# Constants staged and two padding tiles: SBUF start offsets in a fused attention and two-MoE kernel

## The chip, the cores and the metric

One core of a Trainium2 chip runs the whole program. The metric is device time in microseconds (us), the median of three runs.

## The reference

Three steps follow one another on 4608 tokens of 512 features.

```python
# attention: 8 batches x 8 heads, 576 positions of 64 features, softmax inside chunks of 64 positions
attn = softmax(q_c @ k_c.T / 8) ; x = (attn @ v_c)          # x: 4608 x 512
# first MoE: 8 experts 512 -> 1024 -> 512, one expert per token, only tokens with x @ w_skip > 0
e = argmax(x @ w_gate) ; x += gate * (relu(x @ w1[e]) @ w2[e])
# second: dense, 512 -> 2048 -> 512; its weights come as float64
h = x @ w_in ; g = where(h >= 1, h, where(h <= -1, 0, (h + 1)**2 / 4)) ; out = g @ w_out
```

## The kernel before

**Attention and routing** work through 18 units of 256 tokens: q, k and v are loaded by SyncE's DMA queue (`load_qk`, `load_v`), transposed and multiplied on TensorE, and the rows of x are written to DRAM (`xn` to `x_dram`) with a list of tokens for each expert.

**The first MoE** goes expert by expert. An expert's weights come in eight pieces of 128 x 1024 (`piece`): loaded into a staging tile `stg`, then split by ScalarE and VectorE (some by GpSimd) into a high and a low float32r tile. Experts at even places use the pool `wa` (tiles `ah0` to `ah7`, `al0` to `al7`), those at odd places the pool `wb` (`bh*`, `bl*`). `s_M1` makes the hidden features: the weights are the stationary operand, the tokens (`xh`, `xl`) the moving one, 256 to 384 columns of it. `s_M2` makes the output: the hidden features are stationary, the weights move, 512 columns each. In `s_M2` a block of 128 tokens takes 24 matmuls: eight blocks f of hidden features, for each of them (hh, wh), (hh, wl), (hl, wh) as (stationary, moving). The hidden features of f 0 to 3 lie in the pool `h0` (`hh0`, `hl0`, `hh1`, `hl1`), those of f 4 to 7 in the pool `h1` (`hh2` to `hl3`).

**The second MoE** takes nine groups of 512 tokens and for each group 16 blocks m of 128 hidden features. `mm_A` (12 matmuls, output `a`) has the weights `ah*`, `al*` as stationary and the tokens `xh`, `xl` as moving operand; `s_B` (12 matmuls, output `b`, two blocks behind) has the features `gh`, `gl` as stationary and the weights `bh*`, `bl*` as moving operand. ScalarE and VectorE make g of the block in between. In the first group each block also carries one `decode` of a piece of `w_out` from its float64 bits, on VectorE (L189 to L199) and ScalarE.

All matmuls are issued by the helper `mm` (L135) or `tr` (L138), in program order. In a row of the profile `a<-xl,ah` is a matmul into tile a with the operands xl and ah; `mm(o, l, r)` has l as stationary and r as moving operand.

**Where tiles lie.** Pools lie one behind another in each partition of SBUF, in the order in which they are opened, from byte 16512 on; a tile takes a multiple of 32 bytes, and the tile of a closed pool makes room for the next one. The small tiles of the pool `const` come first, among them `cst` (the constants as float32, 677 columns) and `cb` (the first 544 of them as bf16). So the size of `const` sets where every larger tile starts. The rows inside a weight tile, a token tile of 256, 384 or 512 columns and a feature tile are multiples of 512 bytes apart, so that what one matmul reads starts at the same place past a multiple of 512 as its tile.

Of the kernel before, what the change touches and what calls it, by code (L numbers as in the profile page):

```python
# [21 lines left out]
P = 128  # L22
# [64 lines left out]
def kernel(ctx, tc, q, k, v, w_skip, w_gate, w1, w2, w_in, w_out, consts, out):  # L87
# [9 lines left out]
    dec_p = ctx.enter_context(tc.tile_pool(name="dec", bufs=2))  # L97
    ps_moe = ExitStack()
# [8 lines left out]
    cst = const.tile([P, C_ID], F32, name="cst")  # L107
# [13 lines left out]
    ident = const.tile([P, P], F32, name="ident")  # L121
    iota = cb[:, C_IOTA - C_TRI:C_SEL - C_TRI]
# [17 lines left out]
    # ------------------------------------------------ weights  # L140
# [8 lines left out]
    def piece(e, j):  # L149
        """a piece of an expert's weights: loaded, then split"""  # L150
        if j < KD:
            src = w1.rearrange("e (k p) f -> p (e k) f", p=P)[:, bass.ds(ids[e] * KD + j, 1), :]
        else:
            src = w2.rearrange("e (f p) d -> p (e f) d", p=P)[:, bass.ds(ids[e] * (F1 // P) + 2 * (j - KD), 2), :]
        st = stg_p.tile([P, 1024], F32, tag="stg", name="stg")
        halves = [slice(0, 512), slice(512, 1024)]
        for i, cut in enumerate(halves):
            nc.sync.dma_start(out=st[:, cut], in_=src[:, 0, cut] if j < KD else src[:, i])
        yield
        hi, lo = w_t[e, j] = pair(e, j)  # L160
        for cut in halves:
            nc.scalar.copy(out=hi[:, cut], in_=st[:, cut])  # L162
        for cut in halves:
            (nc.vector if e or j == 7 else nc.gpsimd).tensor_tensor(out=lo[:, cut], in0=st[:, cut], in1=hi[:, cut], op=ALU.subtract)  # L164

    # the second half of the hidden features' columns of w_in is split early and waits in DRAM
    m2w = tc.dram_tile([KD, 2, P, 1024], F32R, name="m2w")

    def decode(nm, n, keep=False):
        """a piece of the second MoE's weights: float64 bits into two float32r parts"""  # L170
        if nm == "in":
            kk, c = n % KD, n // KD
            src = w_in[kk * P:kk * P + P, c * 512:c * 512 + 512]
            j, half = kk * 2 + c // 2, c % 2
        else:
            src = w_out[n * P:n * P + P, :]
            j, half = n // 2, n % 2
        cut = slice(half * 512, half * 512 + 512)
        st = (kst_p if keep else stg_p).tile([P, 1024], I32, tag="stg", name="stg")
        nc.sync.dma_start(out=st, in_=src.bitcast(I32))  # L180
        if keep:
            yield
        yield
        v2 = st.rearrange("p (n t) -> p n t", t=2)
        low, top = v2[:, :, 0], v2[:, :, 1]
        a = dec_p.tile([P, 512], I32, tag="a", name="a")
        s = dec_p.tile([P, 512], I32, tag="s", name="s")
        af, sf = a.bitcast(F32), s.bitcast(F32)
        nc.vector.tensor_scalar(out=a, in0=top, scalar1=3, scalar2=0x3FFFFFFF, op0=ALU.logical_shift_left, op1=ALU.bitwise_and)  # L189
        nc.vector.scalar_tensor_tensor(out=a, in0=top, scalar=masks[:, 0:1], in1=a, op0=ALU.bitwise_and, op1=ALU.bitwise_or)  # L190
        nc.vector.tensor_scalar(out=s, in0=a, scalar1=masks[:, 1:2], scalar2=None, op0=ALU.bitwise_and)  # L191
        if keep:
            hl = st.bitcast(F32).rearrange("p (t n) -> p t n", t=2)
            hi, lo = hl[:, 0].bitcast(F32R), hl[:, 1].bitcast(F32R)
        else:
            if (nm, j) not in w_t:
                w_t[nm, j] = pair(0 if nm == "in" else 1, j)
            hi, lo = (t[:, cut] for t in w_t[nm, j])
        nc.vector.scalar_tensor_tensor(out=sf, in0=low.bitcast(U32), scalar=2.0 ** -52, in1=sf, op0=ALU.mult, op1=ALU.mult)  # L199
        yield  # L200
        nc.scalar.copy(out=hi, in_=af)
        nc.gpsimd.tensor_tensor(out=af, in0=af, in1=hi, op=ALU.subtract)
        nc.gpsimd.tensor_tensor(out=lo, in0=af, in1=sf, op=ALU.add)
        if keep:
            nc.gpsimd.dma_start(out=m2w[kk, :, :, cut].rearrange("t p n -> p t n"), in_=hl.bitcast(F32R))
            yield
# [19 lines left out]
    def step(n=1, load=True):  # L226
        """the next pieces of weights, the loads ahead of the arithmetic"""
        for _ in range(n):
            settle()
            if load:  # L230
                ahead()
            if begun:
                next(begun[0], None)
                done.append(begun.pop(0))
# [7 lines left out]
    # ------------------------------------------------ attention and routing  # L242
# [42 lines left out]
    def dve(n=1):  # L285
        """small steps of the routing, put between the large ones"""
        for _ in range(n):
            if fill:
                fill.pop(0)()

    def warm(n, b=None):
        """products that nothing reads keep the tensor engine's clock up while it waits"""
        for _ in range(n):
            mm((big() if b is None else b)[:, 0:512], ones_b, cb[:, 0:512])

    def run(a, b=()):
        """two rows of small steps, by turns"""
        for n in range(max(len(a), len(b))):
            for g in (*a[n:n + 1], *b[n:n + 1]):
                g()  # L300

    def s_T(u, nm):
        """q and k transposed: features of a head pair on the partitions"""
# [22 lines left out]
    def s_SC(u, s):  # L326
        """scores and the numerators of the softmax"""
# [111 lines left out]
    def s_SEL(*us):  # L439
        """logits by token"""  # L440
# [3 lines left out]
        for n, u in enumerate(us):  # L444
            ls = T.pop(("ls", u))
            for s in range(2):
                mm(b[:, 32 * n + 16 * s:32 * n + 16 * s + 16], ls[:, s * P:s * P + P], cst[:, C_SEL:C_SEL + 16])
        return e_SEL(us, b)

    def e_SEL(us, b):  # L450
        """expert, gate and the mask of the computed tokens"""
# [8 lines left out]
        pref = cst[:, C_PREF:C_PREF + NE].rearrange("p (o e) -> p o e", o=1).to_broadcast([P, n, NE])  # L460
# [48 lines left out]
    def s_SNAP(cnt):  # L509
        """the expert that has the most tokens by now is the first: its weights and its list are at hand early"""  # L510
        pref = cst[:, C_PREF:C_PREF + NE]
# [9 lines left out]
    def s_BUMP():  # L521
        """the first expert's first block is closed: later tokens go past it"""
# [7 lines left out]
    def s_RANK(*us):  # L530
        """slot of each computed token in the list of its expert"""
# [41 lines left out]
        def f_put():  # L573
            for s in range(n):
                c = C_TOK + 2 * u + s
# [21 lines left out]
    def s_FIRST():  # L597
        """the first expert's weights"""
# [4 lines left out]
    def s_LIST():  # L603
        """the first expert's list so far"""
# [20 lines left out]
    def s_EARLY():  # L625
        """the first expert's first block, gathered"""
# [15 lines left out]
    def list_last():  # L642
        """the first expert's list: the read part and the later units' tokens"""
# [4 lines left out]
    # ------------------------------------------------ first MoE, by position of an expert  # L648
# [10 lines left out]
    def blocks(j):  # L659
        """the blocks of a position's share: number, first column, rows; the first position's first block goes ahead"""  # L660
# [38 lines left out]
    def s_M1(e, j, between=None):  # L699
        """two blocks of hidden features"""  # L700
# [46 lines left out]
    # the first position's first block, in small steps: the tokens are the weights of the first product  # L747
# [45 lines left out]
    def s_IDX():  # L793
        """the slots' tokens, by position of an expert"""
# [5 lines left out]
    with tc.manual_schedule():  # L800
# [10 lines left out]
        nc.sync.dma_start(out=cst, in_=consts[:, 0:C_ID])  # L811
# [27 lines left out]
        nc.gpsimd.tensor_copy(cb, cst[:, C_TRI:C_SEL])  # L839
# [85 lines left out]
        # the experts by count, the smallest first: their order and their share of the static part  # L925
# [9 lines left out]
        for s in range(4):  # L935
# [3 lines left out]
            out=key, in0=cnt, scalar=float(NE), in1=cst[:, C_PREF:C_PREF + NE], op0=ALU.mult, op1=ALU.add  # L939
        )  # L940
        nc.vector.scalar_tensor_tensor(out=key, in0=ch, scalar=-FAR, in1=key, op0=ALU.mult, op1=ALU.add)
        nc.vector.tensor_tensor(out=t8[r24], in0=key[r24], in1=cst[r24, C_OWN:C_OWN + NE], op=ALU.mult)
# [4 lines left out]
            out=perm, in0=cst[r24, C_POS:C_POS + NL], scalar=own[r24, 1:2], in1=cst[r24, C_BLK:C_BLK + NL], op0=ALU.is_equal, op1=ALU.mult  # L947
        )
        nc.vector.tensor_tensor(out=t8[r24], in0=cnt[r24], in1=cst[r24, C_OWN:C_OWN + NE], op=ALU.mult)
# [7 lines left out]
        mm(bk[0:1, 0:NE], cst[r24, C_E:C_E + 1], heads)  # L957
# [3 lines left out]
        nc.vector.tensor_tensor(out=row[:, 1], in0=row[:, 1], in1=cst[0:1, C_UP:C_UP + NE], op=ALU.add)  # L961
        nc.vector.tensor_scalar(out=order[:, 1], in0=row[:, 1], scalar1=0.0, scalar2=None, op0=ALU.max)
        nc.vector.tensor_scalar(out=order[:, 1], in0=order[:, 1], scalar1=7, scalar2=None, op0=ALU.logical_shift_right)
        nc.vector.tensor_copy(order[:, 2], cst[0:1, C_CAP:C_CAP + NE])
# [22 lines left out]
    # ------------------------------------------------ the tokens past their expert's share, any number of them  # L987
# [57 lines left out]
    def load_x(g, h, a=None):  # L1045
        """half of a group's rows; the first a + 1 blocks of every expert's list hold all that are computed of the first half's block a"""
# [57 lines left out]
    # ------------------------------------------------ second MoE  # L1104
# [33 lines left out]
    def s_A(*gm):  # L1138
        """blocks of hidden features: h, then g(h) = relu(h - 1) + ((clip(h, -1, 1) + 1) / 2)^2"""
# [109 lines left out]
```

## Time and profile before

| | |
|---|---|
| three runs | 1372.41, 1373.9, 1376.27 us; median 1373.9 |
| profiled execution, first to last instruction | 1355.5 us; its time with the launch around it is not listed, the median of the runs is 18.4 us above it |
| TensorE | 1256.8 us busy, granted clock 0.968 of full speed on average |
| VectorE, ScalarE, GpSimd | 727.2, 583.5, 217.2 us busy |

A matmul's busy time is longer than the distance to the next one, since matmuls are pipelined. How fast TensorE really goes is read from the starts of a row of matmuls, or from a piece of the chain that holds a counted number of them: 2.72 us for 12 is one in 226.7 ns. Full speed is 2.4 GHz, where 512 columns take 213.3 ns; at a granted clock of 0.50 it is 1.2 GHz.

### The profile page before, as it was taken

To read this page: it belongs to the slowest core of one execution; us is meant where nothing else is said; L and a number is where in the kernel's file an instruction comes from. 1 tells how busy PE (TensorE), PEld (TensorE's weight loads), DVE (VectorE), ACT (ScalarE), POOL (GpSimd) and SP (SyncE) were. 2 spreads that over 40 slices of the span, in tenths; PEclk is the share of its full clock that TensorE was granted. 3 is DMA by queue.
4 is the path that set the end of the run, shared out by engine and by line. 5 is a ranking of instruction groups with operands and counts; after the bars stand their busy time and mean duration, and the time that the engine had idled before them with its cause. 6 is when DMAs were issued, how large, how long until landed. Compare 5 with 4: busy or idle time off the path is not lost.

```text
span 1355.5 us, 19020 instructions
## 1 busy us (share of the span) xinstructions
PE 1256.8 (93%) x7126; PEld 1054.5 (78%) x7128; DVE 727.2 (54%) x1324; ACT 583.5 (43%) x955; POOL 217.2 (16%) x259
## 2 busy tenths in 40 slices
PE   7877777899989998888999999999999999999998
PEld 6666666689879986666888888888888888888887
DVE  5655557657776697887444444443444444434433
ACT  6756565245444422334434333343443343434433
POOL 3011115623344355433000000000000000000000
PEclk8988888799999998999999999999999999999999
DMA  9889987277866645420101001001010010000000
GB/s 200 188 160 149 161 156 203 76 220 245 263 216 226 209 131 181 157 92 16 47 16 47 16 1 47 16 0 47 16 47 16 0 47 16 32 30 2 32 0 31
DMA packets 123748, 127.41 MB, mean 94 GB/s; under 512 B 46650, under 2 KB 83669, under 8 KB 123654
## 3 DMA queue, kind: packets, MB, share of 16 engines
q1 hardware_dynamic: 114982, 107.40, 30.3%
q0 software_dynamic: 7984, 18.70, 4.3%
q8 instruction: 57, 0.93, 0.3%
q14 instruction: 37, 0.30, 0.1%
q10 hardware_dynamic: 688, 0.07, 0.1%
HBM read 98.14 MB, written 28.73 MB: 94 GB/s over the span
## 4 chain that ended last, share of the span: by engine, by line
PE 62%; DVE 10%; DMA 4%; issue 3%; ACT 1%; POOL 0%; SPq 0%; ACTq 0%; DVEq 0%; POOLq 0%
PE b L135 26%; PE a L135 26%; PE bank L135 4%; PE big L135 4%; DVE a L190 3%; DVE a L189 2%; DMA stg<-in_moe_w_dram 1%; DVE s L191 1%; PE t L138 1%; DMA stg<-in_moe_w_in_dram 1%; DVE r L1160 1%; DVE c L1155 1%; ACT gh L1162 1%; DVE gl L1163 1%; DMA il<-idx_dram 0%
## 5 line engine op out<-in xcount | busy, mean ns | idle before, releaser
L135 PE MATMUL b<-bh,gh 128*128 128x512 f32 x576 | 227.5, 395 | 13.0 <-ACT gh L1162 12.8
L135 PE MATMUL a<-xl,ah 128*128 128x512 f32 (+1 forms) x576 | 225.8, 392 | 3.5 <-DVE xl L1124 3.5
L135 PE MATMUL b<-bh,gl 128*128 128x512 f32 x576 | 226.5, 393 | 0.0
L135 PE MATMUL b<-bl,gh 128*128 128x512 f32 x576 | 224.8, 390 | 0.0
L135 PE MATMUL a<-xh,ah 128*128 128x512 f32 (+1 forms) x576 | 224.6, 390 | 0.0
L135 PE MATMUL a<-xh,al 128*128 128x512 f32 (+1 forms) x576 | 222.8, 387 | 0.0
L1155 DVE SCALAR_TENSOR_TENSOR c<-a,r 128x512 f32<-128x512 f32 x142 | 98.0, 690 | 220.0 <-ACT r L1154 207.1
L1154 ACT ACTIVATE r<-a,bias 128x512 f32<-128x512 f32 x142 | 97.7, 688 | 222.4 <-PE a L135 211.8
L1162 ACT CAST gh<-r 128x512 fp32r<-128x512 f32 x144 | 89.4, 621 | 165.5 <-DVE r L1160 149.4
L1163 DVE TENSOR_TENSOR gl<-r,gh 128x512 fp32r<-128x512 f32 x144 | 100.0, 695 | 110.5 <-ACT gh L1162 110.4
L1160 DVE TENSOR_TENSOR r<-r,c 128x512 f32<-128x512 f32 x144 | 99.8, 693 | 102.2 <-ACT c L1159 102.2
L1159 ACT ACTIVATE c<-c,bias 128x512 f32<-128x512 f32 x144 | 104.4, 725 | 103.8 <-DVE c L1155 103.6
L135 PEld LDWEIGHTS b<-bh,gh 128*128 128x128 f32 x576 | 108.6, 189 | 39.8 <-ACT gh L1162 18.1
L135 PEld LDWEIGHTS b<-bh,gl 128*128 128x128 f32 x576 | 108.5, 188 | 28.2 <-DVE gl L1163 6.0
L135 PEld LDWEIGHTS a<-xl,ah 128*128 128x128 f32 x576 | 108.9, 189 | 25.0 <-DVE xl L1124 3.9
L135 PEld LDWEIGHTS a<-xh,ah 128*128 128x128 f32 x576 | 108.6, 189 | 24.2 <-ACT xh L1123 0.3
L135 PEld LDWEIGHTS a<-xh,al 128*128 128x128 f32 x576 | 108.7, 189 | 23.5
L135 PEld LDWEIGHTS b<-bl,gh 128*128 128x128 f32 x576 | 108.6, 188 | 21.8
L324 ACT COPY qt<-big 64x512 f32<-64x512 f32 x72 | 44.7, 621 | 62.8 <-PE big L138 62.1
L138 PE MATMUL big<-ident,qu 128*128 128x128 f32 x144 | 26.5, 345 | 46.2 <-issue 39.1
L138 PEld LDWEIGHTS big<-ident,qu 128*128 128x128 f32 x144 | 21.2, 178 | 47.4 <-issue 46.7
L164 DVE TENSOR_TENSOR bl<-stg,bh 128x512 fp32r<-128x512 f32 x64 | 46.7, 773 | 6.5 <-ACT bh L162 5.7
(217 smaller groups left out, 2019.2 us busy)
## 6 DMA issues: line engine op xcount, KB each, us to landing
stg<-in_moe_w_dram SPq DMA_DIRECT2D x128, 256.0 KB
vbd<-in_v_dram SPq DMA_DIRECT2D x144, 64.0 KB
out_dram<-o SPq DMA_DIRECT2D x36, 256.0 KB
xs<-x_dram SPq DMA_DIRECT2D x17, 512.0 KB
x_dram<-xn SPq DMA_DIRECT2D x16, 516.0 KB
stg<-in_moe_w_in_dram SPq DMA_DIRECT2D x16, 512.0 KB
stg<-in_moe_w_out_dram SPq DMA_DIRECT2D x16, 512.0 KB
qu<-in_q_dram SPq DMA_DIRECT2D x12, 512.0 KB
```

The lines of the kernel that those rows point to most:

```text
L135: nc.tensor.matmul(out=o, lhsT=l, rhs=r, start=start, stop=stop)
L138: nc.tensor.transpose(out=o, in_=i, identity=ident)
L164: (nc.vector if e or j == 7 else nc.gpsimd).tensor_tensor(out=lo[:, cut], in0=st[:, cut], in1=hi[:, cut], op=ALU.subtract)
L189: nc.vector.tensor_scalar(out=a, in0=top, scalar1=3, scalar2=0x3FFFFFFF, op0=ALU.logical_shift_left, op1=ALU.bitwise_and)
L190: nc.vector.scalar_tensor_tensor(out=a, in0=top, scalar=masks[:, 0:1], in1=a, op0=ALU.bitwise_and, op1=ALU.bitwise_or)
L324: (nc.vector.tensor_copy if eng is nc.vector else nc.scalar.copy)(out=o, in_=b4[64 * r:64 * r + 64, :, par, :])
L1154: nc.scalar.activation(out=r, in_=b, func=ACTF.Relu, bias=bias[:, 0:1])
L1155: nc.vector.scalar_tensor_tensor(out=c, in0=b, scalar=-1.0, in1=r, op0=ALU.max, op1=ALU.subtract)
L1159: nc.scalar.activation(out=c, in_=c, func=ACTF.Square, scale=0.5, bias=bias[:, 1:2])
L1160: nc.vector.tensor_tensor(out=r, in0=r, in1=c, op=ALU.add)
L1162: nc.scalar.copy(out=gh, in_=r)
L1163: nc.vector.tensor_tensor(out=gl, in0=r, in1=gh, op=ALU.subtract)
```

## The change

Of the 677 columns of constants the first 544 are read only once, by the conversion to the bf16 tile `cb`. They now go to the first of the three staging tiles `stg` (named `c0`), and `cst` keeps the other 133 columns. That takes 2176 bytes out of every partition's `const`. Two tiles that nothing reads or writes are added: `even0` (416 bytes, in `const`) and `even1` (960 bytes, in a pool between `dec` and the tiles of attention). Comments and docstrings are gone as well.

```diff
     dec_p = ctx.enter_context(tc.tile_pool(name="dec", bufs=2))
+    ctx.enter_context(tc.tile_pool(name="even", bufs=1)).tile([P, 240], F32, name="even1")
...
-    cst = const.tile([P, C_ID], F32, name="cst")
+    cst = const.tile([P, C_ID - C_SEL], F32, name="cst")
...
     ident = const.tile([P, P], F32, name="ident")
+    const.tile([P, 104], F32, name="even0")
...
-                mm(b[:, 32 * n + 16 * s:32 * n + 16 * s + 16], ls[:, s * P:s * P + P], cst[:, C_SEL:C_SEL + 16])
+                mm(b[:, 32 * n + 16 * s:32 * n + 16 * s + 16], ls[:, s * P:s * P + P], cst[:, 0:16])
...
-        nc.sync.dma_start(out=cst, in_=consts[:, 0:C_ID])
+        c0 = stg_p.tile([P, 1024], F32, tag="stg", name="c0")
+        nc.sync.dma_start(out=c0[:, 0:C_SEL], in_=consts[:, 0:C_SEL])
+        nc.sync.dma_start(out=cst, in_=consts[:, C_SEL:C_ID])
...
-        nc.gpsimd.tensor_copy(cb, cst[:, C_TRI:C_SEL])
+        nc.gpsimd.tensor_copy(cb, c0[:, C_TRI:C_SEL])
```

The other lines of the diff take C_SEL off the column numbers of `cst`. Adding up the pools gives the start of each tile past a multiple of 512 bytes:

| tiles | before | after |
|---|---|---|
| weights `ah*`, `al*`; staging `stg`; `a` of `dec` | 224 | 0 |
| weights `bh*`, `bl*`; attention's `qu`, `ku`, `qt`, `e`, `et` | 288 | 0 |
| tokens `xh`, `xl` of both MoEs; hidden features in `h0`; `r`, `c`, `gh`, `gl` | 288 | 0 |
| hidden features in `h1` | 480 | 192 |
| `xn` (four buffers) | 288, 320, 352, 384 | 0, 32, 64, 96 |
| `xg` (six buffers) | 288 to 448 in steps of 32 | 0 to 160 in steps of 32 |
| `cb`; `ident`; `kbd*` | 288; 352; 352 | 160; 224; 64 |

The order of instructions stays as it was on every engine but for one DMA more. At the start of the program SyncE's queue has the loads of q and k of units 0 to 2 around the constants. Before:

```order
L264 DMA ku<-in_k_dram 128x8x128
L811 DMA cst<-consts_dram 128x677
L264 DMA qu<-in_q_dram 32x8x128
L264 DMA qu<-in_q_dram 96x8x128
L264 DMA ku<-in_k_dram 32x8x128
```

After (lines are three higher at this place):

```order
L266 DMA ku<-in_k_dram 128x8x128
L814 DMA c_157<-consts_dram 128x544
L815 DMA cst<-consts_dram 128x133
L266 DMA qu<-in_q_dram 32x8x128
L266 DMA qu<-in_q_dram 96x8x128
L266 DMA ku<-in_k_dram 32x8x128
```

One DMA has become two, and all later ones of the queue stand one place further back. On GpSimd, near the start, the conversion to `cb` stands where it stood and reads the staging tile. Before:

```order
L823 DMA idx_dram<-dum 128x289
L824 DMA x_dram<-zrow 16x1x32
L825 DMA x_dram<-zrow 4x1x1
L839 CAST cb<-cst 128x544
L380 MEMSET xn 128x2x4 x5
```

After:

```order
L827 DMA idx_dram<-dum 128x289
L828 DMA x_dram<-zrow 16x1x32
L829 DMA x_dram<-zrow 4x1x1
L843 CAST cb<-c_157 128x544
L382 MEMSET xn 128x2x4 x5
```

Nothing moved there; the tile that the conversion reads, and the DMA that it waits for, are others.

## Rows read from the trace of the kernel before

**Rows 1.** The page: the span; busy time, share of the span and instructions of each engine.

```profile
span 1355.5 us, 19020 instructions
PE 1256.8 (93%) x7126; PEld 1054.5 (78%) x7128; DVE 727.2 (54%) x1324; ACT 583.5 (43%) x955; POOL 217.2 (16%) x259
```

**Rows 2.** Busy time by stage: us, engines (instructions), granted clock, DMA share, GB/s.

```profile
0.00:284.00 284.00, 215.74 (x2242) 189.46 (x2244) 159.21 (x535) 158.78 (x282) 72.03 (x105) 0.88 0.81 163
284.00:511.00 227.00, 219.90 (x1222) 195.18 (x1221) 167.24 (x234) 96.94 (x170) 89.53 (x108) 0.98 0.66 216
511.00:634.50 123.50, 103.96 (x471) 78.16 (x470) 104.14 (x123) 41.75 (x70) 52.73 (x45) 0.97 0.37 119
634.50:1355.50 721.00, 717.19 (x3196) 591.73 (x3196) 296.59 (x434) 286.06 (x434) 2.90 (x2) 1.00 0.07 24
```

**Rows 3.** Waits before 290 us: who waited for whom, us, times, longest.

```profile
DVE xn L398 <- DMA x_dram<-xn: 42.1, 12, 6.6
```

**Rows 4.** The chain that ended last, 284 to 511 us: start, us, what.

```profile
284.38 5.56 PE bank L135 x24
...
296.35 11.51 PE big L135 x96
...
325.10 6.81 DMA stg<-in_moe_w_in_dram
...
406.00 16.64 PE big L135 x96
...
463.91 11.09 PE bank L135 x48
```

**Rows 5.** The same chain, 500 to 660 us.

```profile
555.62 0.67 DVE c L1155
...
562.64 0.67 DVE c L1155
...
634.51 4.82 PE b L135 x12
```

**Rows 6.** The same chain, 834 to 848 us.

```profile
834.33 2.75 PE a L135 x12
837.08 2.72 PE b L135 x12
```

**Rows 7.** Busy time in a stretch at 400 us, columns as in rows 2.

```profile
400.00:402.40 2.40, 2.40 (x7) 1.27 (x6) 2.40 (x5) 0.62 (x1) 0.05 (x1) 0.50 1.17 409
```

**Rows 8.** TensorE in order of time, `s_M2` in that stretch: start, us, what.

```profile
400.11 0.63 PE L135 MATMUL bank<-ah,hl 128*64 128x512 f32 x1
...
402.24 0.63 PE L135 MATMUL bank<-al,hh 128*64 128x512 f32 x1
```

**Rows 9.** The same view, `s_M2` with weights of `wb`.

```profile
309.08 0.39 PE L135 MATMUL bank<-bh,hh 128*128 128x512 f32 x1
...
310.44 0.39 PE L135 MATMUL bank<-bh,hh 128*128 128x512 f32 x1
...
312.96 0.39 PE L135 MATMUL bank<-bh,hl 128*128 128x512 f32 x1
```

**Rows 10.** The same view, `s_M2` with weights of `wa`.

```profile
464.21 0.40 PE L135 MATMUL bank<-ah,hl 128*128 128x512 f32 x1
...
466.31 0.39 PE L135 MATMUL bank<-ah,hl 128*128 128x512 f32 x1
...
467.70 0.39 PE L135 MATMUL bank<-ah,hl 128*128 128x512 f32 x1
...
469.06 0.39 PE L135 MATMUL bank<-ah,hl 128*128 128x512 f32 x1
```

**Rows 11.** TensorE in order of time, four bf16 matmuls of `warm`.

```profile
519.83 1.03 PE L135 MATMUL spare<-cb 128*128 128x512 bf16 x4
```

**Rows 12.** All instructions of the tile `spare`: duration ns min/median/max, first and last start.

```profile
L135 PE MATMUL spare<-cb x11: 379/504/631, 516.7 to 520.5; 128*128 128x512 bf16 x11
```

**Rows 13.** The queue of SyncE at the start: start, us of the issue.

```profile
5.57 1.73 SPq L811 DMA_DIRECT2D cst<-consts_dram  x1
```

More of the change, by code (lines that the diff above doesn't have):

```diff
@@ L459, in e_SEL @@
         first = small("first", [P, n, NE])
-        pref = cst[:, C_PREF:C_PREF + NE].rearrange("p (o e) -> p o e", o=1).to_broadcast([P, n, NE])
+        pref = cst[:, C_PREF - C_SEL:C_PREF - C_SEL + NE].rearrange("p (o e) -> p o e", o=1).to_broadcast([P, n, NE])
         fm = small("fm", [P, n, 1])
@@ L509, in s_SNAP @@
     def s_SNAP(cnt):
-        pref = cst[:, C_PREF:C_PREF + NE]
+        pref = cst[:, C_PREF - C_SEL:C_PREF - C_SEL + NE]
         k8, m8 = small("k8", [P, NE], bufs=1), small("m8", [P, 1], bufs=1)
@@ L574, in f_put @@
             for s in range(n):
-                c = C_TOK + 2 * u + s
+                c = C_TOK - C_SEL + 2 * u + s
                 ins = nc.gpsimd.indirect_dma_start(
@@ L938 @@
         nc.vector.scalar_tensor_tensor(
-            out=key, in0=cnt, scalar=float(NE), in1=cst[:, C_PREF:C_PREF + NE], op0=ALU.mult, op1=ALU.add
+            out=key, in0=cnt, scalar=float(NE), in1=cst[:, C_PREF - C_SEL:C_PREF - C_SEL + NE], op0=ALU.mult, op1=ALU.add
         )
         nc.vector.scalar_tensor_tensor(out=key, in0=ch, scalar=-FAR, in1=key, op0=ALU.mult, op1=ALU.add)
-        nc.vector.tensor_tensor(out=t8[r24], in0=key[r24], in1=cst[r24, C_OWN:C_OWN + NE], op=ALU.mult)
+        nc.vector.tensor_tensor(out=t8[r24], in0=key[r24], in1=cst[r24, C_OWN - C_SEL:C_OWN - C_SEL + NE], op=ALU.mult)
         nc.vector.tensor_reduce(out=own[r24, 0:1], in_=t8[r24], axis=AX.X, op=ALU.add)
@@ L946 @@
         nc.vector.scalar_tensor_tensor(
-            out=perm, in0=cst[r24, C_POS:C_POS + NL], scalar=own[r24, 1:2], in1=cst[r24, C_BLK:C_BLK + NL], op0=ALU.is_equal, op1=ALU.mult
+            out=perm, in0=cst[r24, C_POS - C_SEL:C_POS - C_SEL + NL], scalar=own[r24, 1:2], in1=cst[r24, C_BLK - C_SEL:C_BLK - C_SEL + NL], op0=ALU.is_equal, op1=ALU.mult
         )
-        nc.vector.tensor_tensor(out=t8[r24], in0=cnt[r24], in1=cst[r24, C_OWN:C_OWN + NE], op=ALU.mult)
+        nc.vector.tensor_tensor(out=t8[r24], in0=cnt[r24], in1=cst[r24, C_OWN - C_SEL:C_OWN - C_SEL + NE], op=ALU.mult)
         nc.vector.tensor_reduce(out=own[r24, 2:3], in_=t8[r24], axis=AX.X, op=ALU.add)
@@ L956 @@
         heads = perm.rearrange("p (j b) -> p j b", b=NBLK)[:, :, 0]
-        mm(bk[0:1, 0:NE], cst[r24, C_E:C_E + 1], heads)
+        mm(bk[0:1, 0:NE], cst[r24, C_E - C_SEL:C_E - C_SEL + 1], heads)
         mm(bk[0:1, NE:2 * NE], own[r24, 2:3], heads)
@@ L960 @@
         nc.vector.tensor_copy(order[:, 0], row[:, 0])
-        nc.vector.tensor_tensor(out=row[:, 1], in0=row[:, 1], in1=cst[0:1, C_UP:C_UP + NE], op=ALU.add)
+        nc.vector.tensor_tensor(out=row[:, 1], in0=row[:, 1], in1=cst[0:1, C_UP - C_SEL:C_UP - C_SEL + NE], op=ALU.add)
         nc.vector.tensor_scalar(out=order[:, 1], in0=row[:, 1], scalar1=0.0, scalar2=None, op0=ALU.max)
         nc.vector.tensor_scalar(out=order[:, 1], in0=order[:, 1], scalar1=7, scalar2=None, op0=ALU.logical_shift_right)
-        nc.vector.tensor_copy(order[:, 2], cst[0:1, C_CAP:C_CAP + NE])
+        nc.vector.tensor_copy(order[:, 2], cst[0:1, C_CAP - C_SEL:C_CAP - C_SEL + NE])
         nc.vector.tensor_copy(row[:, 3], order[:, 1])
```

## Prediction

> **What bounds the kernel now.** First the page, for the engine with the most work: TensorE is busy for 1256.8 of 1355.5 us [rows 1]. Then busy time by stage, since one share hides four limits [rows 2]. Attention and routing (0 to 284 us) run with the DMA engines busy 0.81 of the time and TensorE at three quarters; VectorE stands for 42.1 us until a store of x rows has landed [rows 3]. In the first MoE (284 to 511 us) the chain that ended last is TensorE's in some pieces, and in others that of the weight supply, a load or a split [rows 4]. From 511 to 634.5 us VectorE is the limit: the chain goes through it, and one block m of the first group takes 7.02 us, from one `c` to the next (555.62 to 562.64) [rows 5], against the 5.47 us that TensorE's two pieces need later. From 634.5 us to the end TensorE stands alone: busy 717.2 of 721.0 us at granted clock 1.00, VectorE 296.6, ScalarE 286.1 [rows 2]. Here a nanosecond of one matmul counts some 3100 times.
>
> So the question is how fast these matmuls go. A piece of 12 with 512 columns takes 2.75 us for `a` and 2.72 us for `b` [rows 6], or 229.2 and 226.7 ns each. At 2.4 GHz, 512 columns are 213.3 ns. Some 13 to 16 ns of each are something else.
>
> **Where those nanoseconds may come from.** Three readings.
>
> - They don't grow with the columns. `s_M1` has 96 matmuls in a piece: 16.64 us with 384 columns and 11.51 us with 256 [rows 4], or 173.3 and 119.9 ns; the columns alone are 160.0 and 106.7. It is 13.3 ns each time, 32 float32 columns.
> - They are gone at half clock. At granted clock 0.50 [rows 7] five matmuls take 2.13 us [rows 8], 426 ns each, and 512 columns at 1.2 GHz are 426.7. So the array doesn't need them; something that keeps pace with a slow array falls behind a fast one, as the fetch of operands would.
> - They depend on where the operands start. In `s_M2` with weights of `wb`, six matmuls from 309.08 to 310.44 us take 226.7 ns each, the next eleven, to 312.96, 229.1 [rows 9]. Nothing changes there but the pool of the stationary operand, from `h0` to `h1`. With weights of `wa` it is the other way round: nine from 464.21 to 466.31 us at 233.3 ns on `h0`, six from 467.70 to 469.06 at 226.7 on `h1` [rows 10].
>
> Set beside the starts (past a multiple of 512) this is a table, stationary then moving: 288 and 288, 226.7 (`b` of the second MoE; `wb` on `h0`); 480 and 224, 226.7 (`wa` on `h1`); 224 and 288, 229.2 (`a`); 480 and 288, 229.1 (`wb` on `h1`); 288 and 224, 233.3 (`wa` on `h0`). Where the two starts are equal or 256 apart it is fastest, and the same pair gives the same time in two stages. So the start offset is felt. The steps are close to multiples of 6.67 ns, the time of 64 bytes of a moving row (16 columns): two of them for the fast pairs, 2.3 and 3 for the others. And all these starts, 224, 288 and 480, are 32 bytes past a multiple of 64: each row that is read touches one piece of 64 bytes more than it fills, the moving one and the stationary one alike. Two pieces are just the 13.3 ns. That is my reading, not a row: no matmul of this kind in the trace has operands at a multiple of 64.
>
> [...]
>
> **The change, part by part.**
>
> *Starts.* Weights, tokens, `h0`, `gh` and `gl` go to 0; so `a`, `b` and `s_M1` get the pair 0 and 0, equal and at a multiple of 64. What is left beyond the columns? Nothing is the lower bound, 213.3 ns. The nearest row with no extra is bf16, half the bytes for as many columns: four of `warm` take 1.03 us [rows 11], less the duration of the last, 379 ns [rows 12], over three: 217 ns. I take 217. The upper bound is 233.3 ns, the worst pair.
>
> - Second MoE: 16 blocks of 144 lie behind at 634.5 us, so that 128 pieces `a` and 130 pieces `b` remain. `a`: 12 x (229.2 - 216.7) = 150 ns, times 128 = 19.2 us. `b`: 12 x (226.7 - 216.7) = 120 ns, times 130 = 15.6 us. Together 35 us. It lies bare: a round of 5.47 us becomes 5.20, and VectorE and ScalarE are busy for about 2.2 us of it.
> - First MoE: TensorE is on the chain with ten pieces of 24 (first and last at 5.56 and, for two, 11.09 us) and three of 96. 24 x 13 ns x 10 = 3.1 us; 96 x 10 ns x 3 = 2.9 us. Some may go into waits for weights behind them, and `h1` goes to 192 beside 0, a pair without a row: I take 5 of 6, bounds 2 and 12 (all 768 + 480 matmuls at 10 ns).
> - 511 to 634.5 us: nothing. VectorE sets the 7.02 us, and TensorE would only wait longer.
> - Attention: its matmuls are float32, not float32r, and stand behind loads; nothing. If loads into aligned tiles are quicker, this stage could gain; no row separates it, and it isn't in the sum.
>
> *Constants.* One DMA of 677 columns becomes two. The bytes are the same, one more issue of at most 1.73 us [rows 13] stands ahead of the loads of unit 1, and the conversion waits for the first of them alone. The loads behind it keep DMA engines busy anyway: nothing, bound +2 us. All other waits and orders are as before; `c0` is read long before the first weights need that staging tile.
>
> *Sum.* 1355.5 - 35 - 5 = 1315.5 us of span; with the 18.4 us between span and median, 1334 us. With 213.3 ns per matmul: `a` 24.4, `b` 20.9, first MoE 12, or 1317. If only one piece of 64 bytes goes (220 ns): `a` 14.1, `b` 10.5, first MoE 2, or 1347.
>
> [...]
>
> **The rivals.**
>
> - *Only the equality of the two starts counts*, and the 13.3 ns are the price of a change of weights. For it: 288 with 288 and 480 with 224 are both at 226.7. Against: it vanishes at half clock. Then `a` falls to 226.7: 12 x 2.5 ns x 128 = 3.8 us, and `wa` on `h0` gains some 1 us: 1369 us.
> - *Nothing happens*: the pairs of the table are also pairs of pools, and what sets 226.7 and 233.3 ns apart may be something of the pools that padding doesn't touch. For it: all starts in the table are 32 past a multiple of 64, so that no row has one of the kind that is to come. Against: `a` and `wb` on `h1` share no pool pair and agree within 0.1 ns. [...]
> - *Slower*: the moving read and the weight read now both begin on a multiple of 512 and meet at the same place at once. [...] Against: in the table equal starts are the best. Priced at the worst pair, 233.3 ns: `a` 6.3, `b` 10.3, first MoE 3, so 1394 us. It decides from 228 ns per matmul on, today's mean.
> - *Attention gets quicker too*: 1329 or less; part of the first case's range.
>
> **How the numbers follow.** My forecast (both pieces go, or at least one) 0.63, own range 1317 to 1347. Equality alone 0.14, nothing 0.11, slower 0.12. 0.3% (4 us) is what this kernel's runs can tell from no change; equality alone lies on that line, so half of it counts as faster: 0.70 faster; the other half and nothing, 0.18, same; 0.12 slower. The range must reach over equality alone and half of nothing to leave out no more than 2 in 10: 1316 to 1373 us.
>
> **What would show it.** In the chain after 634 us, pieces of 12 at 2.60 us for `a` and `b` alike, rounds of 5.20 us; the 384-column pieces of 96 at 15.7 us; 426 ns still at half clock; the block of 7.02 us unchanged, with TensorE waiting longer in it; `s_M2` different between `h0` and `h1` if 192 beside 0 is a bad pair. If `a` and `b` are both 2.72, equality was all. If they are above 2.74 us, the prediction has the wrong sign.

## The result, and the profile after

| | runs | median us | lowest to highest |
|---|---|---|---|
| before | 6 | 1371.39 | 1367.01 to 1376.27 |
| after | 6 | 1356.72 | 1353.69 to 1362.53 |

The ratio is 0.991, 95% interval 0.988 to 0.9939: a gain of 12 to 15 us, where 40 were forecast. The sign was right, the size was a third. The profiled execution has a span of 1351.9 us, and its own time is 1353.69: only 1.8 us lie around the span. So the execution of before that was profiled, with its span of 1355.5 us, took some 1357 us: 14 less than the median, less than any of the six runs listed, and near this kernel's medians in the sessions of the experiments below (1358.3 to 1360.5). The two traces together cannot show the whole gain.

Busy time by stage after, columns as in [rows 2]:

```profile
0.00:284.00 284.00, 215.21 (x2245) 188.45 (x2247) 162.84 (x535) 158.78 (x283) 74.34 (x107) 0.89 0.76 165
284.00:511.00 227.00, 219.83 (x1215) 195.29 (x1215) 167.88 (x233) 97.30 (x170) 88.54 (x106) 0.98 0.66 214
511.00:634.50 123.50, 104.08 (x473) 78.83 (x472) 104.45 (x123) 41.60 (x69) 52.55 (x46) 0.97 0.37 119
634.50:1351.90 717.40, 713.54 (x3196) 591.56 (x3196) 296.44 (x434) 285.98 (x435) 2.90 (x2) 1.00 0.07 24
```

The last stage holds the same 3196 matmuls and is 3.6 us shorter (721.0 to 717.4). The three stages ahead of it look alike, but their windows have fixed ends and hide a shift. All copies into attention's `et` and all hidden features `hh` of the first MoE on ScalarE (duration ns min/median/max, first and last start), before:

```profile
L369 ACT COPY et<-big x18: 585/585/605, 22.6 to 230.4; 128x512 f32<-128x512 f32 x18
L713 ACT ACTIVATE hh<-big x32: 588/651/815, 273.6 to 492.2; 128x512 fp32r<-128x512 f32 x16, 128x768 fp32r<-128x768 f32 x12, 128x640 fp32r<-128x640 f32 x4
```

After:

```profile
L371 ACT COPY et<-big x18: 585/585/605, 19.4 to 225.7; 128x512 f32<-128x512 f32 x18
L715 ACT ACTIVATE hh<-big x32: 587/648/820, 263.1 to 492.7; 128x512 fp32r<-128x512 f32 x16, 128x768 fp32r<-128x768 f32 x12, 128x640 fp32r<-128x640 f32 x4
```

Attention ends 4.7 us earlier, the last hidden features come no earlier: from the last `et` to the last `hh` it is 267.0 us instead of 261.8. In the traces of all the runs below this stretch takes 259 to 269 us, with no order by the starts, so that one pair of traces can hide what attention gains. One number moves in the first stage: the DMA engines are busy 0.76 of it instead of 0.81, at 165 GB/s instead of 163. About the same bytes take less of the engines' time.

The chain of work that ended last, 834 to 848 us, which answers to [rows 6]:

```profile
836.00 2.72 PE b L137 x12
838.72 2.72 PE a L137 x12
```

`a` and `b` are alike, and both at 226.7 ns. What should have gone to 217 stayed where `b` had been. The prediction named this sign: "If `a` and `b` are both 2.72, equality was all."

The same chain in the first MoE and in the first group of the second, which answer to [rows 4, 5]:

```profile
296.86 11.51 PE big L137 x96
...
555.93 0.67 DVE c L1159
...
562.94 0.67 DVE c L1159
```

`s_M1` with 256 columns takes 11.51 us as before: 119.9 ns each, 13.3 above the columns, though its operands now start at 0 and 0. (That a column costs 1 / 2.4 GHz is an estimate from [rows 4]: 128 columns more lengthen 96 matmuls from 11.51 to 16.64 us, 0.417 ns a column.) The block of VectorE is 7.01 us (7.02 before).

That piece has weights of `wb`, whose start was equal to that of the tokens before, too (288 and 288). With weights of `wa` (224 and 288 before) the same 96 matmuls became slower. TensorE in order of time, the first matmul of such a piece and the first behind it, before:

```profile
319.55 0.28 PE L135 MATMUL big<-xh,ah 128*128 128x256 f32 x1
...
330.85 0.40 PE L135 MATMUL bank<-ah,hh 128*128 128x512 f32 x1
```

After:

```profile
320.07 0.28 PE L137 MATMUL big<-xh,ah 128*128 128x256 f32 x1
...
331.58 0.40 PE L137 MATMUL bank<-ah,hh 128*128 128x512 f32 x1
```

That is 117.7 ns each before and 119.9 after: with 256 columns equal starts are the slower pair. With 384 columns the starts made no difference: the piece of `wa` at 440.42 us of before took 16.64 us like that of `wb` in [rows 4].

TensorE in order of time, `s_M2` with weights of `wb`, which answers to [rows 9]; `h0` up to 310.73, then `h1`:

```profile
309.14 0.39 PE L137 MATMUL bank<-bl,hh 128*128 128x512 f32 x1
...
310.73 0.39 PE L137 MATMUL bank<-bh,hl 128*128 128x512 f32 x1
310.96 0.39 PE L137 MATMUL bank<-bh,hh 128*128 128x512 f32 x1
...
312.79 0.39 PE L137 MATMUL bank<-bh,hl 128*128 128x512 f32 x1
```

Seven from 309.14 to 310.73 are 227 ns each, eight from 310.96 to 312.79 are 229 each. So 0 beside 0 is worth what 288 beside 288 was; 192 beside 0 what 480 beside 288 was. The rows of 512 columns at full clock that were read, before and after, fit one rule: only the moving start less the stationary start counts, as a remainder by 256. At 0 it is 226.7 ns, at 64 it is 229.1, at 192 it is 233.3. The rule is one of 512 columns: at 256 the pair at 64 was the quicker one.

Last, the wait that stood in [rows 3]: who waited for whom before 290 us, total us, times, longest.

```profile
DVE xn L400 <- DMA x_dram<-xn: 38.9, 9, 6.8
```

It is 3.2 us less, in 9 instances instead of 12.

### The profile page after: what moved, and what is told of

Read it like the earlier page. It is cut to its first block, busy times and chain, and to the rows that moved or that the text cites. A ratio compares the mean times of both kernels' runs of the same rounds, so it can differ in the third digit from the quotient of the medians.

```text
span 1351.9 us, 19022 instructions
## 1 busy us (share of the span) xinstructions
PE 1252.7 (93%) x7126; PEld 1054.1 (78%) x7128; DVE 731.6 (54%) x1324; ACT 583.7 (43%) x955; POOL 218.3 (16%) x259
## 4 chain that ended last, share of the span: by engine, by line
PE 74%; DVE 11%; issue 5%; DMA 4%; ACT 4%; POOL 1%; SPq 0%; ACTq 0%; POOLq 0%; DVEq 0%
PE b L137 26%; PE a L137 26%; PE bank L137 9%; PE big L137 7%; PE big L140 5%; DVE a L192 3%; DVE a L191 2%; ACT qt L326 2%; DMA stg<-in_moe_w_dram 1%; PE t L140 1%; DVE s L193 1%; DMA idx_dram<-cst,si 1%; DVE r L1164 1%; DVE acc L555 1%; DVE c L1159 1%
## 5 line engine op out<-in xcount | busy, mean ns | idle before, releaser
L137 PE MATMUL a<-xh,ah 128*128 128x512 f32 (+1 forms) x576 | 223.2, 388 | 0.0
L137 PE MATMUL a<-xh,al 128*128 128x512 f32 (+1 forms) x576 | 223.2, 388 | 0.0
```

What stands on the lines that cost most here:

```text
L137: nc.tensor.matmul(out=o, lhsT=l, rhs=r, start=start, stop=stop)
```

## The experiments

The rows explain 3.6 us of TensorE. For the rest there were two theories. **A**: there are two gains, equal starts on TensorE, and loads that are quicker into attention's tiles, which the padding moved as well (q and k from 288 to 0). **B**: the pair of starts is all, and the rest is spread between executions. Padding can be given to the stages apart. No experiment changes what is computed. The ratio is to the kernel before in the same session (medians there 1359.9, 1360.5, 1358.3 and 1360.0 us). The DMA share is that of the first 200 us. Attention's end is the start of the last copy into `et`, in us; it and the next two columns come from one execution each. The last column is counted from the trace's packet records: how many of the 36867 packets of 512 bytes (q and k) before 230 us took over 1.15 of their usual 27 ns.

| run | q, k at | PE starts | ratio, interval | attention's end | DMA share | slow packets |
|---|---|---|---|---|---|---|
| e1 before again | 288 | 224/288 | 0.9996, 0.9979 to 1.0012 | 236.7 | 0.93 | 41% |
| e2 after, attention + 32 | 32 | equal | 0.9963, 0.9944 to 0.9982 | 236.6 | 0.88 | 41% |
| e3 before, attention at 0 | 0 | 224/288 | 0.9913, 0.9888 to 0.9938 | 223.2 | 0.83 | 13% |
| e4 after, all + 32 | 32 | equal | 0.9986, 0.9973 to 1.0 | 235.3 | 0.89 | 41% |
| e5 after again | 0 | equal | 0.9921, 0.9897 to 0.9944 | 227.7 | 0.84 | 13% |
| e6 after, attention + 64 | 64 | equal | 0.9972, 0.9954 to 0.9989 | 232.0 | 0.93 | 41% |
| e7 before, q and k alone | 0 | 224/288 | 0.9947, 0.9928 to 0.9966 | 226.7 | 0.82 | 11% |
| e8 before, the rest alone | 288 | 224/288 | 0.9996, 0.9977 to 1.0014 | 231.6 | 0.93 | 43% |
| f2 after, attention + 128 | 128 | equal | 0.9935, 0.991 to 0.996 | 231.9 | 0.94 | 35% |
| f3 after, attention + 256 | 256 | equal | 0.9922, 0.9901 to 0.9944 | 223.8 | 0.82 | 10% |
| g1 before, q and k + 96 | 384 | 224/288 | 0.9986, 0.9969 to 1.0004 | 230.2 | 0.93 | 35% |

**The two stages apart: e1 to e4.** e1 is the kernel before, unchanged.

> The kernel before, once more. Theory A (two gains: the pair of starts on TensorE, and quicker transfers into attention's aligned tiles): a second profile has a span of 1355 to 1375 us, pieces of 12 at 2.75 (a) and 2.72 us (b), and when its span is the longer one the difference lies ahead of 284 us. Theory B (only the pair of starts; the other 11 us between the medians are spread between executions): the same pieces, and here too a median within 4 us of 1357.

It repeats its kernel (0.9996). Its trace is 7.3 us longer than the first one of before, and 6.3 us of that lie ahead of attention's end (236.7 for 230.4); by itself this fits both theories. Its median, 1360.9 us, is some 10 us under that of the same kernel in the first session (1371.4), so that only ratios within a session are compared.

e2 is the changed kernel with 32 bytes ahead of attention's tiles; those pools are closed before the second MoE, whose tiles stay where they are.

```diff
     attn = ExitStack()
+    attn.enter_context(tc.tile_pool(name="padq", bufs=1)).tile([P, 8], F32, name="padq")
     qk_p = attn.enter_context(tc.tile_pool(name="qk", bufs=2))
```

> The changed kernel with attention's tiles (q, k, v, x and so on) 32 bytes further, at 32 past a multiple of 512 instead of 0; all else at 0 as in the changed kernel. Theory A: the transfers into attention lose their gain, the pieces of 12 stay at 2.72 us for a and b: 3 to 5 us faster than before (ratio 0.997). Theory B: as fast as the changed kernel whatever attention's starts are (ratio 0.991).

e3 is the kernel before with the same line and `[P, 56]`, 224 bytes.

> The kernel before with attention's tiles alone 224 bytes further, at 0 past a multiple of 512 as in the changed kernel; weights, tokens and features stay at 224 and 288. Theory A: 8 to 12 us faster than before (ratio 0.992 to 0.994), with pieces of 2.75 and 2.72 us as before, and 512-byte packets of q and k nearer to their least duration. Theory B: the same as before within 0.2% (ratio 0.998 to 1.002).

e4 is the changed kernel with 32 bytes more behind the constants, so that weights, tokens and attention's tiles all stand at 32.

```diff
-    const.tile([P, 104], F32, name="even0")
+    const.tile([P, 112], F32, name="even0")
```

> The changed kernel with everything from the weights on 32 bytes further: weights, staging, tokens and attention all at 32 past a multiple of 512, so equal starts that are not at a multiple of 64. Both theories for TensorE: 2.72 us for a and b alike, since only the distance of the two starts counts. Theory A: ratio 0.997, the transfers lose their gain. Theory B: ratio 0.991 like the changed kernel. If a and b rise over 2.75 us, a multiple of 64 counts on TensorE after all.

e3, with TensorE's starts as before, gains as much as the whole change: 0.9913. e2, which differs from the changed kernel in attention's tiles alone, gains less than half of that: 0.9963. e4, with equal starts at 32 past a multiple of 64, has hardly a gain: 0.9986. B falls. The chain of e3, 834 to 848 us, shows that nothing was gained on TensorE there:

```profile
836.28 2.75 PE a L135 x12
839.02 2.72 PE b L135 x12
```

and that of e4 that equal starts do at 32 what they do at 0, so the multiple of 64 had no part in it:

```profile
836.29 2.72 PE b L137 x12
839.01 2.72 PE a L137 x12
```

Where e3's gain lies is seen in the first 200 us, columns as in [rows 2]. First e1, then e3:

```profile
0.00:200.00 200.00, 149.93 (x1685) 133.04 (x1687) 107.67 (x356) 125.12 (x218) 32.49 (x61) 0.91 0.93 169
```

```profile
0.00:200.00 200.00, 156.36 (x1744) 138.97 (x1747) 113.57 (x385) 130.32 (x228) 34.70 (x65) 0.90 0.83 175
```

In the same 200 us every engine gets further, TensorE by 59 instructions, and more is moved (175 GB/s for 169) with the DMA engines less busy (0.83 for 0.93). Attention's last copy into `et` comes 13.5 us earlier. e1, then e3:

```profile
L369 ACT COPY et<-big x18: 585/585/605, 22.9 to 236.7; 128x512 f32<-128x512 f32 x18
```

```profile
L370 ACT COPY et<-big x18: 585/585/605, 19.3 to 223.2; 128x512 f32<-128x512 f32 x18
```

**Which tiles, and which remainder: e5 to e8.** e5 is the changed kernel again.

> The changed kernel once more, beside the next three and the kernel before on the same chip. If two gains add (equal starts on TensorE, and attention's tiles at a multiple of 512), it stands at about 0.988 to 0.991 of the kernel before, below the kernel with attention's tiles alone at 0 (0.991), by up to 4 us. If attention's tiles are all of it, exactly at that 0.991.

If two gains add, it should stand below e3's 0.9913. It came at 0.9921, with an interval that overlaps that of e3, so the times alone don't show that the two gains add up. TensorE's part is read from the last stage (3.6 us).

e6 is e2 with `[P, 16]`, 64 bytes.

> The changed kernel with 64 bytes ahead of attention's tiles, so that q and k land at 64 past a multiple of 512; all else as changed. If what the transfers want is a start at a multiple of 64 bytes, it stands with the changed kernel (within 2 us), and the share of q's and k's packets above the least duration is 13%. If they want more (256 or 512), it stands with the one that had 32 bytes there, 8 to 12 us slower than the changed kernel, and the share is 41%.

e7 and e8 part attention's tiles in the kernel before: in e7 q and k alone come to 0 (what lies behind them moves by 256 bytes), in e8 all but q and k move, by the 224 bytes of e3.

```diff
     attn = ExitStack()
+    attn.enter_context(tc.tile_pool(name="padq", bufs=1)).tile([P, 56], F32, name="padq")
     qk_p = attn.enter_context(tc.tile_pool(name="qk", bufs=2))
+    attn.enter_context(tc.tile_pool(name="padr", bufs=1)).tile([P, 8], F32, name="padr")
```

> The kernel before with only the tiles of q and k at 0 past a multiple of 512 (224 bytes ahead of them, 32 behind, so that what follows keeps its remainder by 64, 32). If q's and k's transfers are the gain of the aligned attention, all of it: 0.991 of the kernel before, 8 to 12 us. If it is another tile of attention (v, x, the operands of its matmuls), 1.000.

```diff
     qk_p = attn.enter_context(tc.tile_pool(name="qk", bufs=2))
+    attn.enter_context(tc.tile_pool(name="padr", bufs=1)).tile([P, 56], F32, name="padr")
```

> The other half: q and k stay at 288 past a multiple of 512, all tiles of attention behind them move by 224 bytes, as in the kernel that gained. If q's and k's transfers are the gain: 1.000 of the kernel before. If it is what lies behind them: 0.991.

q and k are the place: 0.9947 with them alone, 0.9996 with all the others. Attention ends at 226.7 us in e7 and at 231.6 in e8. The gain of e7 is smaller than the 0.991 that was expected; its interval just overlaps that of e3, and whether the other tiles add something once q and k are at 0 stays open. The transposes that read q and k on TensorE are not what became quicker: those of k and q take 26.1 and 26.9 us in e7, 26.5 and 25.2 in e1. The first 200 us of e7, of e8, and of e6:

```profile
0.00:200.00 200.00, 153.58 (x1718) 137.92 (x1720) 112.29 (x378) 127.99 (x223) 33.93 (x64) 0.89 0.82 175
```

```profile
0.00:200.00 200.00, 149.80 (x1701) 133.70 (x1702) 108.19 (x359) 126.52 (x220) 32.48 (x61) 0.90 0.93 171
```

```profile
0.00:200.00 200.00, 150.68 (x1701) 134.82 (x1702) 108.14 (x359) 127.21 (x220) 32.52 (x61) 0.90 0.93 170
```

e6 shows that 64 is not enough: a DMA share of 0.93 like that of e8, and a gain (0.9972) about as large as TensorE's 3.6 us, 0.9974.

**Which power of two: f2, f3, g1.** f2 and f3 are e2 with `[P, 32]` and `[P, 64]`.

> The changed kernel with attention's tiles (q and k first) at 128 past a multiple of 512. If the transfers want 512 or 256: as with 64 bytes there, 0.997 of the kernel before, and 41% of q's and k's packets above the least duration. If 128 does: 0.992 and 13%.

> The same at 256 past a multiple of 512. If the transfers want a multiple of 256: 0.992 of the kernel before and 13%. If they want 512: 0.997 and 41%.

By share, packets and attention's end 256 is as good as 0, and 128 is about as bad as 32. By the time f3 agrees (0.9922), but f2 does not: at 0.9935 it is quicker than TensorE's gain alone. g1 asked again, without a gain on TensorE: e7 with other sizes, q and k at 384, which is 128 past a multiple of 256 (what lies behind them moves by 128 bytes).

```diff
     attn = ExitStack()
+    attn.enter_context(tc.tile_pool(name="padq", bufs=1)).tile([P, 24], F32, name="padq")
     qk_p = attn.enter_context(tc.tile_pool(name="qk", bufs=2))
+    attn.enter_context(tc.tile_pool(name="padr", bufs=1)).tile([P, 8], F32, name="padr")
```

> The kernel before with only q's and k's tiles moved, from 288 to 384 past a multiple of 512 (128 past a multiple of 256), nothing gained on TensorE. If the share of DMA time is the cause (it was 0.94 of the first 200 us at 128, as at 32 and 64, against 0.82 at 0 and 256): 1.000 of the kernel before, and again about 0.93. If a multiple of 128 is enough for the time, whatever the share: 0.995, as with q and k at 0.

The time is that of the kernel before (0.9986, interval over 1) and the share is 0.93. So of the starts tried only the multiples of 256 gain. With q and k there, attention ends between 223.2 and 227.7 us in the table; with all other starts, between 230.2 and 236.7. The first 200 us of f3, and of g1:

```profile
0.00:200.00 200.00, 156.49 (x1734) 140.29 (x1735) 112.56 (x379) 129.85 (x225) 34.67 (x65) 0.90 0.82 175
```

```profile
0.00:200.00 200.00, 151.28 (x1702) 134.59 (x1703) 108.95 (x363) 126.79 (x220) 32.62 (x62) 0.90 0.93 172
```

Why f2 was about 5 us quicker than e6 stays open. In its trace the first 200 us are like e6's, and attention ends as late (231.9 and 232.0 us). Its profiled execution is quicker behind that, in the stretch that varies from trace to trace. Hidden features of f2, then of e6:

```profile
L716 ACT ACTIVATE hh<-big x32: 591/648/815, 275.0 to 490.6; 128x512 fp32r<-128x512 f32 x16, 128x768 fp32r<-128x768 f32 x12, 128x640 fp32r<-128x640 f32 x4
```

```profile
L716 ACT ACTIVATE hh<-big x32: 588/650/817, 268.0 to 494.2; 128x512 fp32r<-128x512 f32 x16, 128x768 fp32r<-128x768 f32 x12, 128x640 fp32r<-128x640 f32 x4
```

**What a float32r matmul costs: f1.** Behind the last product of the changed kernel stand 17 groups of 24 products that nothing reads.

```diff
             if n >= LAG:
                 s_B(*seq[n - LAG])
+        hi = [w_t["out", j][0] for j in range(2)]
+        X = x2_t[NG - 1][0].rearrange("p k n -> p (k n)")
+        tb = (tri, ones_b)
+        sweep = [
+            *((f"z{32 * i + 0}", lambda n, i=i: (hi[n % 2][:, 0:P], X[:, 8 * i:8 * i + GT])) for i in range(9)),
+            ("y64_64", lambda n: (hi[n % 2][:, 16:16 + P], X[:, 16:16 + GT])),
+            ("y64_0", lambda n: (hi[n % 2][:, 16:16 + P], X[:, 0:GT])),
+            ("samew", lambda n: (hi[0][:, 0:P], X[:, 0:GT])),
...
```

> The changed kernel with groups of 24 products behind its last one, which nothing reads, each between two weight tiles by turns (so the whole time is some 90 us longer and only the rows of these groups count). z0 to z256: float32r, 512 columns, the stationary operand at 0, the moving one at 0, 32, ... 256 bytes past it. By the rule of distances: 226.7 ns at 0 and 256, 229.1 at 64, 233.3 at 192. By my old reading (extra pieces of 64 bytes): z32, z96, z160, z224 slower than z0 and z64 by 6.7 ns each. y64_64 against z0: the same by the rule of distances; y64_0 as z192. samew (the same weights each time): 213 to 217 if the 13.3 ns are the price of a change of weights, 226.7 if they belong to float32r itself. w64 and w32 (64 and 32 stationary columns): shorter than 226.7 if the 13.3 ns is the time in which weights are brought in. k64: half the rows. bfsame and bfturn: bf16 with the same weights and by turns; 217 for the first, and for the second 217 if the 13.3 ns come with float32 operands, 226.7 if any change of weights costs them.

The chain in one stretch of 2.7 us within each group: start, us, what, how many. In order of time they are z0, z32, z64, z96, z128, z160, z192, z224, z256, y64_64, y64_0, samew, w64, w32, k64, bfsame, bfturn (the trace leaves the figures of names out).

```profile
1335.64 2.95 PE z L137 x13
1341.58 2.80 PE z L137 x12
1346.93 2.98 PE z L137 x13
1352.69 2.80 PE z L137 x12
1358.30 2.80 PE z L137 x12
1363.90 2.81 PE z L137 x12
1369.52 2.80 PE z L137 x12
1375.11 2.80 PE z L137 x12
1381.15 2.95 PE z L137 x13
1386.86 2.95 PE y L137 x13
1391.42 3.03 PE y L137 x13
1397.48 2.95 PE samew L137 x13
1402.48 2.99 PE w L137 x13
1408.01 3.01 PE w L137 x13
1414.22 2.95 PE k L137 x13
1419.47 3.02 PE bfsame L137 x14
1424.65 3.02 PE bfturn L137 x14
```

Time by count: 227 ns at distances 0 and 256 and for 64 beside 64; 229 at 64; 233 to 234 at 32, 96, 128, 160, 192, 224 and for 64 beside 0. My old reading, 6.7 ns more for each start that is 32 past a multiple of 64, falls: z128 and z192 have both starts at multiples of 64 and are as slow as z32. The same weights each time (samew) are 227, so it isn't the change from one weight tile to another. They are loaded again for every matmul, though, as TensorE in order of time shows, so that a price of each load isn't ruled out:

```profile
1396.62 2.21 PE L137 MATMUL samew<-xh,bh 128*128 128x512 f32 x9
1396.85 1.78 PEld L137 LDWEIGHTS samew<-xh,bh 128*128 128x128 f32 x8
```

With 64 and 32 stationary columns it is 230 and 231.5, not less; with half the rows (k64) 227. bf16 is 215.7 ns, 2.4 above the columns, with the same weights and by turns. So at 512 columns some 11 of the 13.3 ns come with the float32r operands, and no start that was tried takes them away; by what means they come stays open.

## Why the prediction was wrong

- **Where the size failed: "What is left beyond the columns? Nothing is the lower bound, 213.3 ns. The nearest row with no extra is bf16 ... I take 217."** The step ahead of it read 13.3 ns as two extra pieces of 64 bytes, because all starts of the trace were 32 past a multiple of 64. No row had another start, so that a constant looked like an effect of the one thing that never varied. By that reading all pairs of its table should have cost the same two pieces; they took 226.7 to 233.3 ns, and its own count of 2.3 pieces for one of them was a sign against it. That operands come in pieces of 64 bytes, and that their fetch falls behind at full clock, was an estimate of mine that no run shows. f1, e4 and the rows after show the 13.3 ns at 512 columns with every pair of equal starts that was tried, 0, 32 and 64. The bf16 row was near in columns but differed in the type, and the type carries some 11 of the 13.3 ns. Of `a`'s 19.2 us the 3.8 of the equality rival came, of `b`'s 15.6 nothing: 3.6 us together.
- **The rival "only the equality of the two starts counts" was right for the second MoE**, with its 3.8 us against 3.6 measured. Its explanation, a price for the change of weights, has no support in samew; a price of each load stays open. That starts are felt at all, which the prediction read from 226.7, 229.1 and 233.3 ns, holds.
- **"It is 13.3 ns each time" was read from pieces with equal starts or 384 columns.** The piece of `wa` with 256 columns in the same trace took 117.7 ns, 11.0 above the columns, at unequal starts. So equality isn't always the best pair.
- **First MoE, -5 us: no gain is seen.** The pieces of 96 are as long as before or, in `wa` with 256 columns, 0.2 us longer; `s_M2` with weights of `wb` is as before (226.7 and 227 ns on `h0`, 229.1 and 229 on `h1`).
- **511 to 634.5 us, nothing: right**, 7.01 us a block against 7.02.
- **Attention: "If loads into aligned tiles are quicker, this stage could gain; no row separates it, and it isn't in the sum."** This was the larger part of the real gain. By e7 it is some 7 us (0.9947), by e3 some 12 (0.9913). e7 and TensorE's 3.6 us together give 0.9947 x 0.9974 = 0.9921, which is e5's ratio; with e3 it would be 0.9887, below each of the three ratios at hand (0.991, 0.9921, 0.9922), so that the size of this part is known only between the two. [Rows 2] had the lead: the stage kept the DMA engines busy for 0.81 of its time, so that a cheaper packet could show in its length. The packet records of the trace before hold the rest: of q's and k's packets 41% took well over 27 ns.
- **At which starts packets are slow** the prediction did not ask. The runs agree in where it turns: 10 to 13% slow packets at 0 and 256, 35 to 43% at 32, 64, 128, 288 and 384. The usual packet takes 27 ns at 288 (the trace before) and at 0 (the trace after) alike, so that the means stay open.
- **Constants, nothing:** no run separates them, but e4, which has them and equal starts, is not slower than the kernel before (0.9973 to 1.0), and TensorE's gain would cover at most 3.6 us.
- **"the 18.4 us between span and median"** lay between executions, not around the span, which is 1.8 us. It could be kept as a constant for the difference, but the span of before was no middling one.
- **The slower rival**, two reads that meet at the same place, has no support at 512 columns: 0 beside 0 is among the fastest pairs, 227 ns (z0 in f1) against 229 to 234 at the distances from 32 to 224. No run shows two reads that meet.

## What to carry to other kernels

Where a stage keeps the DMA engines busy (0.81 of attention here), put the tiles that its small packets land in at multiples of 256 bytes: of the packets of 512 bytes 10 to 13% were slow there, 35 to 43% at the other starts tried, and a few hundred bytes of padding gave 7 to 12 us (e7, e3). For float32r with 512 columns give the stationary and the moving tile the same start by 256; of 0, 32 and 64 none was better than another (227 ns each), and it is worth 1 to 3% of matmul time (229 to 234 ns at the other distances tried). With 256 columns measure first: there equal starts cost 2% (119.9 ns for 117.7). And where a property is the same in every row that a reading rests on, the rows can't say that it is the cause: a row in which it differs has to be made first.

## What the hardware showed that was not expected

- Float32r with 512 columns: 226.7 ns at best, 213.3 for the columns; bf16 215.7. It is the same 13.3 ns at 256 columns with equal starts (11.51 us for 96), but 11.0 with the stationary operand at 224 and the moving one at 288 (117.7 ns).
- At 512 columns the distance of the starts by 256 sets the rest: 0 gives 226.7, 64 gives 229, all others tried (steps of 32) 233 to 234 (the trace after and f1).
- Behind a change of operands the first matmuls were slower before they settled, at equal starts too: the first seven of samew in f1 took 231 ns each on average and the thirteen behind them 227; in the trace after, the first four of `s_M2` from 308.21 us took 232 and the next seven 227. So rates are read from rows further in.
- Fewer stationary columns are slower, not quicker: 230 ns with 64 and 231.5 with 32 (w64 and w32 in f1), 227 with 128.
- q's and k's starts slow v's packets as well: with q and k alone at a new remainder by 256 (e7; what lies behind them moved by just 256 bytes), 14% of v's 256-byte packets took over 1.15 of their usual 18 ns, against 40% in the trace before and 47% in e1.
